# A table of 242 moves behind the planner's order of an attention and expert-layer kernel

## The chip, the cores and the metric

One core of one Trainium2 chip runs the whole program. The metric is the device time of one execution in microseconds (us), the median of several runs. TensorE (PE) does the matmuls, VectorE (DVE), ScalarE (ACT) and GpSimd (POOL) the rest of the arithmetic; SyncE (SP) issues every transfer of this kernel.

## The reference

Attention over 4 batches, 8 heads, 768 positions and 64 dimensions: each query sees its window of positions less than 16 away, and 24 blocks of 32 positions, by the largest key and the mean value of each. A gated layer over all 3072 tokens follows (512 to 1536 to 512).

```python
    k_sum = k.reshape(B, H, nb, block, D).max(axis=3)
    v_sum = v.reshape(B, H, nb, block, D).mean(axis=3)
    scale = 1.0 / np.sqrt(D)
    scores_l = scale * np.matmul(q, k.transpose(0, 1, 3, 2))
    mask_l = np.abs(pos[:, None] - pos[None, :]) < window
    scores_s = scale * np.einsum('bhsd,bhnd->bhsn', q, k_sum)
    scores_s = scores_s + np.log(block)
    scores_l_m = np.where(mask_l, scores_l, -1000000000.0)
    scores_all = np.concatenate([scores_l_m, scores_s], axis=-1)
    scores_all = scores_all - np.max(scores_all, axis=-1, keepdims=True)
    a = np.exp(scores_all)
    a = a / (np.sum(a, axis=-1, keepdims=True) + 1e-09)
    v_all = np.concatenate([v, v_sum], axis=2)
    return np.matmul(a, v_all).astype(np.float32)
...
    g = x @ w_gate
    silu = g * (1.0 / (1.0 + np.exp(-g)))
    val = x @ w_val
    return (silu * val @ w_out).astype(np.float32)
```

`block` is 32 and `window` 16; x is the output of the attention, one row for each token.

## The kernel before

Tokens are worked on in halves of a batch, 384 each: half k = 0 and 1 are batch 0, 2 and 3 are batch 1, and so on. A unit (k,u) is the attention of two heads (u = 0 to 3) in half k. Its steps carry names: SC(k,u) scores on TensorE; max, scl or ttr0 and ttr1 the row maxima with the mask on DVE; exp0 to exp5 on ScalarE; eps a tiny addition to the sums, rcp their reciprocal; nrm the product of probabilities and reciprocals (128x720, L708, on DVE or POOL); PP0 and PP1 the transposes on TensorE into PSUM, pt0 and pt1 their copies to SBUF; XO the product with the values (L762); xh and xl the split of x into a high and a low part, since every product of float32 is made of three matmuls of parts.

For half 0 the values come out of one tile vn of the values as they lie in memory. odd1(u) and odd2(u) copy shifted rows of it into the window tile vw, and val1(u) and val2(u) copy the block means (24 rows) into vw and vn; all four are copies of 384 columns (L465 on POOL or DVE, L463 on ACT) and XO(0,u) reads what they write. Later halves load windows of values, and values(k,u) copies the means into them (24x768); join does the same for keys, pool and vpool make the maxima and sums of blocks.

The weights of the expert layer arrive in 12 pieces each of gate and value together (w0 to w11) and of output (o0, o2, ...), as 64-bit floats that are decoded to float32: raw_w is the load (128x2048, 1024 KB), then abs (ACT, L941), clamp, shift, sign and low (DVE, L945 to L964, 128x1024), then hi (ACT, a cast, L463) and lo (DVE or POOL, the remainder, L468) for the matmuls. keep_w stores a decoded piece, wa, sf, la, ls and again_w are later transfers of weights and of sums. sumA22, sumA21, sumA12 and sumA11 are sums of 256-wide parts of a decoded piece (L468).

g(j,h) and v(j,h) are the gate and value matmuls of piece j for half h of batch 0 (L1105); silu, mul, hh and hl make the activation and its two parts, D0 and D1 multiply by the output weights, part adds up. Batches 1 to 3 use seven products of sums in place of eight plain ones (P1 to P7, L1147).

What sets the order: every operation is a Step of a Plan, with a cost on each engine that may do it. `order` (L273) works out when each step is wanted and lets `run` (L308) place the steps one by one; a table `NUDGES` shifts the wanted times by hand and names engines. In `run`, a step of POOL or DVE that doesn't read PSUM is held until 0.2 us before the end of such a step on the other of the two (`held`, L361 to L402). The steps come back sorted by their planned start, and the loop at L1469 issues them so; `after` chains each engine's instructions in this order. All transfers stand in one queue, that of SyncE. In the first 110 us of the plan, `warm_up` (L1257) puts up to 30 matmuls on a tile of zeros ahead of a TensorE step for which the plan shows idle time.

Of the kernel before, what the change touches and what calls it, by code (L numbers as in the profile page):

```python
# [80 lines left out]
PE, DVE, ACT, POOL, DMA = "PE", "d", "a", "p", "q"  # L81
# [174 lines left out]
def nudge(steps, late):  # L256

    by = {s.name.replace(" ", "_"): s for s in steps}
    for line in NUDGES.replace("\n", ";").split(";"):
        if not line.strip():  # L260
            continue
        name, *what = line.split()
        s = by[name]
        for x in what:
            if x[0] in "+-":
                late[s] += float(x)
            elif x[0] == "s":
                s.slack = float(x[1:])
            else:
                s.engines = {x: s.engines[x]}  # L270


def order(steps):  # L273

    for s in steps:
        s.next = []
    for s in steps:
        for o in s.after:
            o.next.append(s)
    pe = [s for s in steps if PE in s.engines]  # L280
    line = [[s for s in pe if s.side == x] for x in range(2)]
    wanted = {}
    t = 6.0
    for s in pe:
        wanted[s] = t
        t += s.engines[PE]
    for _ in range(3):
        late = {}
        for s in reversed(steps):
            x = wanted.get(s, 1e9)  # L290
            for o in s.next:
                x = min(x, late[o] - (LAG.get(o_engine(s), 0.07) if s.after is not None else 0))
            late[s] = x - min(s.engines.values(), default=0)
        run(steps, line, late)
        wanted = {s: s.start + s.engines[PE] for s in pe}
        for s in line[1]:
            if s.gate is not None:
                wanted[s] = min(wanted[s], s.gate.end + EARLY)
    nudge(steps, late)
    run(steps, line, late)  # L300
    return sorted(steps, key=lambda s: (s.start, s.n))


def o_engine(s):
    return next(iter(s.engines), None)
# [106 lines left out]
def body(ctx, tc, qP, kP, kW, vT, vW, vN, vR, wgv, wo, bias, out):  # L412
    nc = tc.nc

    def after(x, y):

        tc.add_manual_dep(
            x, y.name, mybir.DependencyInfo(mybir.DependencyClass.NoSync, mybir.DependencyReason.DATA), reason="order"
        )
# [10 lines left out]
    def make(buf):  # L430
        if buf.tile is None:
            buf.tile = pools[buf.ring.pool][1].tile(
                buf.shape, buf.dtype, tag=buf.ring.tag, bufs=buf.ring.bufs, name=buf.name
            )
        return buf.tile
# [9 lines left out]
    plan = Plan()  # L445
# [27 lines left out]
    spare = [0]  # L473
# [66 lines left out]
    KT, KS, VT, VR, Q, KWD, VW, PR, PT, ST, XO, VN = ({} for _ in range(12))  # L540
# [538 lines left out]
    def silu(name, a, src, reads):  # L1079
        plan.add(  # L1080
            name, {ACT: 0.49}, lambda e: nc.scalar.activation(out=make(a), in_=src(), func=AF.Silu), reads, (a,), table="silu"  # L1081
        )
# [383 lines left out]

    traced = nc.cur_bb.bb.instructions
    last = {}
    for s in order(plan.steps):  # L1469
        if s.engine == PE and s.start < 110.0:  # L1470
            spare[0] = min(30, max(0, int((s.idle - 0.5) / 0.25)))
        n = len(traced)
        if s.engine is None:
            s.do()
        else:
            s.do(s.engine)
        spare[0] = 0
        for x in traced[n:]:
            if x.engine in last:
                after(x, last[x.engine])  # L1480
            last[x.engine] = x
# [45 lines left out]
```

## Time and profile before

| what | us |
|---|---|
| median of 3 runs | 677.97 |
| lowest and highest | 676.67, 678.21 |
| the profiled execution | 678.46 |
| its span | 676.8 |
| TensorE busy in it | 662.9 |
| DVE busy in it | 498.9 |

The profiled execution is one run like the others, taken with the hardware profiler. Its span goes from the first to the last instruction; 1.66 us of its time lie around it. An engine's busy time counts its instructions, so idle time of TensorE is what the order around it can change.

### The profile page before, as it was taken

The page shows a single profiled execution, that of the slowest core. Times are in us where ns is not written, and L with a number is a line of the kernel's source. Part 1 is how long each engine was busy: PE and PEld are TensorE (multiplying, and loading weights), DVE is VectorE, ACT ScalarE, POOL GpSimd, SP SyncE. Part 2 cuts the span into 40 slices and gives each one's busy share as a digit, 9 for nine tenths or more (in the row PEclk, how much of TensorE's full clock was granted, in tenths as well). Part 3 has the DMA queues.
Part 4 walks back from the last instruction along what each step waited for, and adds up shares of the span by engine and source line. Part 5 has one row for each costly group of instructions (what it writes and reads, how often), then busy time and mean ns, then how long its engine had stood idle before and what let it go on. Part 6 is the DMA issues. An engine that isn't in the chain of part 4 may idle for free.

```text
span 676.8 us, 13318 instructions
## 1 busy us (share of the span) xinstructions
PE 662.9 (98%) x5077; PEld 611.0 (90%) x5077; DVE 498.9 (74%) x1073; ACT 373.5 (55%) x901; POOL 130.7 (19%) x141
## 2 busy tenths in 40 slices
PE   8799999999999999999999999999999999999997
PEld 8699899899898899989898998989999898989896
DVE  5899998999979685967689674766658761646464
ACT  4877758868654576545645386754635243413130
POOL 4303113235225020145413100201003000000000
PEclk9999999999999999999999999999999999999999
DMA  9997668869964686886657484663726362626232
GB/s 345 365 383 283 221 242 284 289 234 354 324 227 167 254 305 222 315 284 219 241 205 253 155 303 150 222 214 112 249 72 211 144 251 73 239 88 222 106 110 93
DMA packets 39681, 152.71 MB, mean 226 GB/s; under 512 B 4352, under 2 KB 8896, under 8 KB 32704
## 3 DMA queue, kind: packets, MB, share of 16 engines
q1 hardware_dynamic: 39616, 151.85, 63.3%
q8 instruction: 40, 0.66, 0.4%
q14 instruction: 25, 0.20, 0.1%
HBM read 116.18 MB, written 35.65 MB: 224 GB/s over the span
## 4 chain that ended last, share of the span: by engine, by line
PE 84%; DMA 8%; DVE 5%; SPq 1%; ACT 1%; issue 1%; POOL 0%; DVEq 0%; POOLq 0%
PE p L1147 35%; PE acc L1219 28%; PE g L1105 6%; PE v L1105 6%; DMA s<-ss 3%; PE xo L762 3%; DMA raw_o<-in_wo 3%; PE pp L729 2%; PE sc L610 2%; DMA s<-sf 1%; DMA vn<-in_vN 1%; SPq L482 1%; DVE p L708 0%; DVE nm L663 0%; DVE o L468 0%
## 5 line engine op out<-in xcount | busy, mean ns | idle before, releaser
L1219 PE MATMUL acc<-o,hh 128*128 128x512 f32 x570 | 178.0, 393 | 0.0
L1219 PEld LDWEIGHTS acc<-o,hh 128*128 128x128 f32 x570 | 105.4, 188 | 22.1 <-issue 1.3
L1147 PE MATMUL p<-xh_T,s 128*128 128x384 f32 x432 | 122.5, 338 | 0.9 <-DMA s<-ss 0.8
L1219 PE MATMUL acc<-o,hl 128*128 128x512 f32 x285 | 111.5, 391 | 0.0
L1147 PE MATMUL p<-xh_B,wa 128*128 128x384 f32 x288 | 84.9, 335 | 0.0
L1147 PEld LDWEIGHTS p<-xh_T,s 128*128 128x128 f32 x432 | 79.0, 188 | 3.2 <-DMA s<-ss 2.0
L463 ACT CAST hh<-a 128x384 fp32r<-128x384 f32 x73 | 37.5, 514 | 70.1 <-DVE a L468 67.3
L463 ACT COPY s<-p 128x384 f32<-128x384 f32 x64 | 30.7, 479 | 75.5 <-PE p L1147 75.1
L1147 PE MATMUL p<-xl_T,s 128*128 128x384 f32 x216 | 72.3, 335 | 0.0
L468 DVE TENSOR_TENSOR part<-acc,part 128x512 f32<-128x512 f32 x71 | 47.2, 684 | 27.0 <-PE acc L1219 27.0
L1219 PEld LDWEIGHTS acc<-o,hl 128*128 128x128 f32 x285 | 53.5, 188 | 11.8 <-DVE hl L468 0.3
L468 DVE TENSOR_TENSOR hl<-a,hh 128x384 fp32r<-128x384 f32 x84 | 49.3, 586 | 14.0 <-ACT hh L463 11.2
L653 ACT ACTIVATE p<-p,nm 128x120 f32<-128x120 f32 x144 | 55.1, 384 | 2.5 <-DVE nm L641 2.2
L468 DVE TENSOR_TENSOR c<-p,u 128x384 f32<-128x384 f32 x72 | 39.7, 552 | 22.7 <-PE p L1147 22.6
L1105 PE MATMUL g<-xh_B,w 128*128 128x384 f32 x192 | 53.7, 338 | 0.0
L1105 PE MATMUL v<-xh_B,w 128*128 128x384 f32 x192 | 53.4, 337 | 0.0
L1147 PEld LDWEIGHTS p<-xh_B,wa 128*128 128x128 f32 x288 | 53.0, 188 | 0.1
L1147 PE MATMUL p<-xl_B,wa 128*128 128x384 f32 x144 | 48.1, 334 | 0.0
L1147 PE MATMUL p<-xh_B,s 128*128 128x384 f32 x144 | 42.6, 336 | 1.0 <-DVE v L468 1.0
L1147 PE MATMUL p<-xh_T,wa 128*128 128x384 f32 x144 | 42.3, 334 | 0.0
L468 DVE TENSOR_TENSOR a<-c,a 128x384 f32<-128x384 f32 x65 | 36.2, 557 | 7.1 <-ACT a L1081 4.1
L1147 PEld LDWEIGHTS p<-xl_T,s 128*128 128x128 f32 x216 | 40.6, 188 | 0.3
(161 smaller groups left out, 1353.3 us busy)
## 6 DMA issues: line engine op xcount, KB each, us to landing
wa<-wa SPq DMA_DIRECT2D x36, 768.0 KB, 4.3
s<-ss SPq DMA_DIRECT2D x24, 1024.0 KB, 7.3
raw_w<-in_wgv SPq DMA_DIRECT2D x12, 1024.0 KB, 7.4
ss<-s SPq DMA_DIRECT2D x12, 1024.0 KB, 7.2
wa<-w SPq DMA_DIRECT2D x12, 768.0 KB, 6.0
kw<-in_kW SPq DMA_DIRECT2D x24, 360.0 KB, 5.6
vw<-in_vW SPq DMA_DIRECT2D x28, 288.0 KB, 4.6
kt<-in_kP SPq DMA_DIRECT2D x16, 400.0 KB, 5.4
```

Of the source, the lines that this page charges most:

```text
L463: nc.scalar.copy(out, in_)
L468: vector[e].tensor_tensor(out=out, in0=a, in1=b, op=op)
L482: plan.add(name, {DMA: moved(name, nbytes)}, lambda e: nc.sync.dma_start(out(), in_()), reads, writes)
L610: nc.tensor.matmul(make(sc[h])[s * QT : (s + 1) * QT, c * KC + at : c * KC + at + x.shape[-1]], make(q)[hs, qs], x, start=not biased or c ...
L653: nc.scalar.activation(out=make(p)[:, i, :], in_=make(p)[:, i, :], func=AF.Exp, scale=-1.0, bias=make(nm)[:, i : i + 1], accum_out=make(sm ...
L729: nc.tensor.transpose(make(pp)[:KC, c * P : (c + 1) * P], make(p)[:, g * NT // 2 + c, :], make(id_sb))
L762: nc.tensor.matmul(ps[hs, qs], v, make(pt)[:, h, qs], start=True, stop=True)
L1105: nc.tensor.matmul(t[:, :TOK], a, x, start=u == order_of[0] and i == 0, stop=u == order_of[-1] and i == 2,)
L1147: nc.tensor.matmul(t[:, :TOK], a, x, start=first and kk == 0 and n == 0, stop=kk == 1 and n == 2, skip_group_check=not first,)
L1219: nc.tensor.matmul(ps[:, :wide], a, w, start=j == js[0] and m == 0, stop=j == js[-1] and m == 2)
```

## The change

After the planner has its order, `moved_behind` takes each engine's list of steps out of it and goes through a table of 242 pairs: of a pair `x y`, step x is taken out of its engine's list and put directly behind y. 102 pairs are on DVE, 54 on ScalarE, 44 in the transfer queue, 21 on TensorE and 21 on POOL; no step changes its engine, and nearly all belong to the first third of the run. Then one common order is made of the lists again, by rank and by what each step needs. The rule for warm-up matmuls is replaced by a table: 14 of them instead of 21, at SC(0,1), PP0(0,2) and PP1(0,2). No step is added, removed or computed in another way. ScalarE's order has 44 table loads in place of 46, because steps that use the same table stand together more often. The lines of the functions below the table are 75 higher in the changed kernel.

```diff
+WARM = {"SC(0,1)": 5, "PP0(0,2)": 8, "PP1(0,2)": 1}
+
+MOVES = (
...
+    "vpool(1,3) part(0,1,5); mul(6,0) sign_w8; vpool(2,0) mul(6,0); hh(0,6,0) vpool(2,0); low_w8 low_w9; "
...
+    "odd2(2) val2(0); val2(2) odd2(2); val1(2) val2(2); values(1,1) eps(1,1); sumA22_w3 eps(1,3); sumA11_w2 sumA22_w3; "
...
+)
+
+def moved_behind(out):
+
+    lists = {}
+    for i, s in enumerate(out):
+        s.rank = i
+        lists.setdefault(s.engine, []).append(s)
+    named = {s.name.replace(" ", "_"): s for s in out}
+    for pair in MOVES.split("; "):
+        x, y = (named[n] for n in pair.split())
+        line = lists[x.engine]
+        line.remove(x)
+        line.insert(line.index(y) + 1, x)
+    marks = set(lists.pop(None, []))
+    done, again = set(), []
+    while marks or any(lists.values()):
+        heads = [l[0] for l in lists.values() if l] + list(marks)
+        s = min((h for h in heads if all(o in done for o in h.after)), key=lambda h: h.rank)
+        if s.engine is None:
+            marks.remove(s)
+        else:
+            lists[s.engine].pop(0)
+        done.add(s)
+        again.append(s)
+    return again
...
-    for s in order(plan.steps):
-        if s.engine == PE and s.start < 110.0:
-            spare[0] = min(30, max(0, int((s.idle - 0.5) / 0.25)))
+    for s in moved_behind(order(plan.steps)):
+        if s.engine == PE:
+            spare[0] = WARM.get(s.name, 0)
```

The first place is the transfer queue at the start. In a row, `kt`, `q` and `vn` are keys, queries and values of half 0, `raw_w0` to `raw_w3` weight pieces, `vw_1_0` window values of half 1. Before:

```order
L482 DMA kt_0_2_229<-in_kP 128x800
L482 DMA raw_w0_234<-in_wgv 128x2048
L482 DMA raw_w3_299<-in_wgv 128x2048
L482 DMA q_0_2_320<-in_qP 128x384
L482 DMA raw_w1_333<-in_wgv 128x2048
L482 DMA vw_1_0_371<-in_vW 96x768
L482 DMA vw_1_1_376<-in_vW 96x768
L482 DMA raw_w2_416<-in_wgv 128x2048
```

Changed:

```order
L557 DMA kt_0_2_223<-in_kP 128x800
L557 DMA raw_w0_228<-in_wgv 128x2048
L557 DMA vn0_230<-in_vN 128x1536
L557 DMA vn0_230<-in_vR 32x256
L557 DMA q_0_2_310<-in_qP 128x384
L557 DMA raw_w1_316<-in_wgv 128x2048
L557 DMA vw_1_0_351<-in_vW 96x768
L557 DMA raw_w2_356<-in_wgv 128x2048
```

The load of piece w3 has left this place: it stands behind raw_w2, the load raw_o0 and the store keep_w1, seven rows below the end of this list. The values vn0 now come behind piece w0.

The second place is POOL from about 15 to 31 us. `vw_0_u` and `vn` are the value tiles of unit (0,u) and `vs_0` the block means, so `vw_0_2<-vn1` is odd2(2), `vw_0_2<-vs_0` val1(2), `vn1<-vs_0` val2(2), `vw_0_0<-vs_0` val1(0) and `vn0<-vs_0` val2(0); the row of L708 is nrm(0,2). Before:

```order
L465 COPY vw_0_2_323<-vn1_119 32x384
L465 COPY vw_0_2_323<-vs_0_296 24x384
L465 COPY vn1_119<-vs_0_296 24x3x128
L465 COPY vw_0_1_255<-vs_0_296 24x384
L465 COPY vw_1_1_376<-vs_0_296 24x768
L465 COPY vw_0_0_464<-vn0_184 64x384
L465 COPY vw_0_0_464<-vn0_184 32x384
L465 COPY vw_0_0_464<-vs_0_296 24x384
L465 COPY vn0_184<-vs_0_296 24x3x128
L708 TENSOR_TENSOR p_0_2_468<-p_0_2_468,ri_0_2_518 128x720
```

Changed:

```order
L540 COPY vw_0_3_321<-vn1_116 32x384
L540 COPY vw_0_0_442<-vn0_230 32x384
L540 COPY vw_0_3_321<-vs_0_293 24x384
L540 COPY vn1_116<-vs_0_293 24x3x128
L783 TENSOR_TENSOR p_0_2_449<-p_0_2_449,ri_0_2_503 128x720
L540 COPY vw_0_0_442<-vs_0_293 24x384
L540 COPY vn0_230<-vs_0_293 24x3x128
L540 COPY vw_0_2_490<-vn1_116 32x384
L540 COPY vn1_116<-vs_0_293 24x3x128
L540 COPY vw_0_2_490<-vs_0_293 24x384
```

val1(0), val2(0) and the three copies of unit (0,2) stood ahead of nrm(0,2) and now stand behind it; those of unit (0,3) follow odd2(0) at the top of the second list.

The third place is DVE at about 146 to 153 us, around the decoding of pieces w8 and w9. `m_w9<-raw_w9` of the last two decode lines are sign and low, `w8<-m_w8` is lo w8, `vw_3_0<-vs_1` values(3,0), and the ISA rows are ttr0(3,0). Before:

```order
L964 SCALAR_TENSOR_TENSOR m_w8_1847<-raw_w8_1553,m_w8_1847 128x1024
...
L468 TENSOR_TENSOR w8_1990<-m_w8_1847,w8_1990 128x1024
L468 TENSOR_TENSOR hl_0_6_1_2015<-a_0_6_1_1926,hh_0_6_1_2008 128x384
L468 TENSOR_TENSOR a_0_7_0_2013<-v_7_0_1993,a_0_7_0_2013 128x384
L951 TENSOR_SCALAR m_w9_1970<-m_w9_1970 128x1024
L465 CAST hh_0_7_0_2034<-a_0_7_0_2013 128x384
L958 SCALAR_TENSOR_TENSOR m_w9_1970<-raw_w9_1633,m_w9_1970 128x1024
L832 TENSOR_REDUCE vr_2_0_2054<-vt_2_0_1853 128x24
L964 SCALAR_TENSOR_TENSOR m_w9_1970<-raw_w9_1633,m_w9_1970 128x1024
L465 COPY vw_3_0_2071<-vs_1_1646 24x768
L641 ISA p_3_0_2124,nm_3_0_2125<-sc0_3_0_2074,bias_sb_825 128x120
```

Changed:

```order
L1033 SCALAR_TENSOR_TENSOR m_w9_1955<-raw_w9_1657,m_w9_1955 128x1024
L1039 SCALAR_TENSOR_TENSOR m_w9_1955<-raw_w9_1657,m_w9_1955 128x1024
L1039 SCALAR_TENSOR_TENSOR m_w8_1819<-raw_w8_1505,m_w8_1819 128x1024
L543 TENSOR_TENSOR a_0_7_0_2013<-v_7_0_1972,a_0_7_0_2013 128x384
L540 COPY vw_3_0_2106<-vs_1_1636 24x768
L716 ISA p_3_0_2109,nm_3_0_2110<-sc0_3_0_2052,bias_sb_807 128x120
...
L543 TENSOR_TENSOR w8_2085<-m_w8_1819,w8_2085 128x1024
```

low w8 has gone from eleven rows ahead of low w9 to the row behind it, and lo w8 from ahead of the steps of w9 to behind values(3,0) and ttr0(3,0). On POOL, hl(0,7,0) stood ahead of lo w9 and is now behind it.

## Rows read from the trace of the kernel before

**Rows 1.** The page: the span, TensorE's busy time, the clock granted to TensorE in 40 equal slices (tenths of full speed), and the chain of work that ended last, by engine.

```profile
span 676.8 us, 13318 instructions
...
PE 662.9 (98%) x5077; PEld 611.0 (90%) x5077; DVE 498.9 (74%) x1073; ACT 373.5 (55%) x901; POOL 130.7 (19%) x141
...
PEclk9999999999999999999999999999999999999999
...
PE 84%; DMA 8%; DVE 5%; SPq 1%; ACT 1%; issue 1%; POOL 0%; DVEq 0%; POOLq 0%
```

**Rows 2.** Busy time by stretch: the stretch, its length, busy time and instructions of TensorE, its weight loads, DVE, ACT and POOL, TensorE's granted clock, the share of the transfer engines, GB/s.

```profile
0.00:36.50 36.50, 29.87 (x471) 26.79 (x472) 27.67 (x50) 24.68 (x78) 13.65 (x28) 1.00 0.97 359
36.50:75.00 38.50, 37.38 (x446) 33.95 (x445) 37.83 (x60) 31.29 (x82) 10.90 (x10) 1.00 0.82 303
...
151.00:162.00 11.00, 11.00 (x115) 10.77 (x110) 10.87 (x35) 10.69 (x27) 5.50 (x6) 1.00 0.96 320
...
220.40:245.00 24.60, 23.60 (x174) 22.73 (x173) 18.20 (x56) 16.46 (x41) 4.50 (x6) 1.00 0.75 266
```

**Rows 3.** TensorE's waits from 0 to 245 us: the waiting line, what it waited for, us in total, how often, the longest.

```profile
PE pp L1260 <- ACT pt L463: 1.9, 1, 1.9
PE sc L610 <- DMA q<-in_qP: 1.4, 2, 0.9
...
PE p L1147 <- DVE v L468: 1.0, 1, 1.0
...
PE pp L729 <- DVE p L708: 0.7, 1, 0.7
```

**Rows 4.** The timeline around lo w9 and values(3,0) and (3,1): start and length in us, engine, line, operation, shape. The first POOL row is another step of the same shape (lo w6).

```profile
152.43 0.56 DVE L465 COPY vw<-vs 24x768 f32<-24x768 f32 x1
154.96 2.05 DVE L465 COPY vw<-vs 24x768 f32<-24x768 f32 x1
...
126.55 2.41 POOL L468 TENSOR_TENSOR w<-m_w,w 128x1024 fp32r<-128x1024 f32 x1 [7.25 <-ACT w L463]
153.99 2.59 POOL L468 TENSOR_TENSOR w<-m_w,w 128x1024 fp32r<-128x1024 f32 x1 [2.73 <-ACT w L463]
```

**Rows 5.** The timeline of POOL's copies of values and of nrm(0,2), and DVE's low w0, from 20 to 31 us.

```profile
20.52 0.69 POOL L465 COPY vw<-vs 24x384 f32<-24x384 f32 x1 [3.32 <-ACT vs L463]
22.05 1.06 POOL L465 COPY vw<-vn 64x384 f32<-64x384 f32 x1
23.16 1.39 POOL L465 COPY vw<-vn 32x384 f32<-32x384 f32 x1
25.06 0.51 POOL L465 COPY vn<-vs 24x384 f32<-24x384 f32 x1
29.47 1.39 POOL L708 TENSOR_TENSOR p<-p,ri 128x720 f32<-128x720 f32 x1 [3.90 <-DVE ri L705]
...
22.66 1.52 DVE L964 SCALAR_TENSOR_TENSOR m_w<-raw_w,m_w 128x1024 int32<-128x1024 int32 x1
```

**Rows 6.** The page's row of the loads of gate and value pieces (KB each, us from issue to landing), and the timeline of rcp(0,2), of the decoding after it (clamp w2), of XO(0,2)'s second part and of the first matmul of g(0,0).

```profile
raw_w<-in_wgv SPq DMA_DIRECT2D x12, 1024.0 KB, 7.4
...
29.13 0.19 DVE L705 RECIPROCAL ri<-sm 128x6 f32<-128x6 f32 x1
33.68 0.69 DVE L945 TENSOR_SCALAR m_w<-m_w 128x1024 f32<-128x1024 f32 x1 [1.41 <-ACT m_w L941]
...
34.45 0.27 PE L762 MATMUL xo<-pt,vw 120*64 120x64 f32 x1
35.28 0.44 PE L1105 MATMUL g<-xh_B,w 128*128 128x384 f32 x1
```

**Rows 7.** The view of the decoded pieces' tile on POOL (the 256-wide sums: shortest, median and longest in ns), and the timeline of rcp(1,3) and of POOL's hl for another step.

```profile
L468 POOL TENSOR_TENSOR m_w<-m_w x9: 729/1250/1713, 55.3 to 105.0; 128x256 f32<-128x256 f32 x9
...
71.78 0.19 DVE L705 RECIPROCAL ri<-sm 128x6 f32<-128x6 f32 x1
...
67.84 1.01 POOL L468 TENSOR_TENSOR hl<-a,hh 128x384 fp32r<-128x384 f32 x1 [2.50 <-ACT hh L463]
```

**Rows 8.** The timeline of ScalarE's abs w1, hi w5, a table load and an exponential, of DVE's lo w5, and of the first matmul of g(5,0).

```profile
23.94 1.15 ACT L941 ACTIVATE m_w<-raw_w 128x1024 f32<-128x1024 f32 x1 [1.10 <-DMA raw_w<-in_wgv]
...
99.47 1.06 ACT L463 CAST w<-m_w 128x1024 fp32r<-128x1024 f32 x1 [2.89 <-DVE m_w L964]
103.47 1.28 ACT L653 ACT_TABLE_LOAD   x1
104.76 0.40 ACT L653 ACTIVATE p<-p,nm 128x120 f32<-128x120 f32 x1
...
101.08 1.21 DVE L468 TENSOR_TENSOR w<-m_w,w 128x1024 fp32r<-128x1024 f32 x1
...
107.84 0.33 PE L1105 MATMUL g<-xh_B,w 128*128 128x384 f32 x1
```

**Rows 9.** The timeline of DVE's lo w8, low w9 and the first of three parts of ttr0(3,0), and of the first matmul of g(8,0).

```profile
146.13 1.21 DVE L468 TENSOR_TENSOR w<-m_w,w 128x1024 fp32r<-128x1024 f32 x1
151.18 1.21 DVE L964 SCALAR_TENSOR_TENSOR m_w<-raw_w,m_w 128x1024 int32<-128x1024 int32 x1
153.02 0.28 DVE L641 CUSTOM_DVE_ANT_0 p<-sc,bias_sb 128x120 f32<-128x120 f32 x1
...
154.91 0.33 PE L1105 MATMUL g<-xh_B,w 128*128 128x384 f32 x1
```

41 rows, old and new, of the table MOVES are left out of this document.

## The prediction

> **What bounds the kernel now.** I read the page first: TensorE is busy for 662.9 of 676.8 us, at a granted clock of 9 tenths or more in every slice (the higher of its two levels, 2.4 GHz), and the chain that ended last is 84% TensorE, with transfers second at 8% and VectorE (DVE) third at 5% [rows 1]. So the time can only change where TensorE waits. The busy times by stretch show where that is. From 0 to 36.5 us TensorE is busy 29.87 us; part of the rest is the start, before the first data. From 36.5 to 75 it lacks 1.12 us, from 75 to 220.4 nothing (the stretch 151 to 162 stands for it), and from 220.4 to 245 just 1.00 [rows 2]. TensorE's waits name what was late: 1.9 us before the transposes of unit (0,2), 0.7 for the probabilities of (1,3), 1.0 for one value product at 236 us, 1.4 in all for queries q [rows 3]. The moves lie in the first third, so they can win at most the waits in this list that they touch, and they can lose wherever a step that had time to spare now has none. DVE is the engine to watch: busy 37.83 of 38.50 us in the second stretch and 10.87 of 11.00 in 151 to 162, almost as full as TensorE [rows 2].
>
> **A price that the sum needs.** GpSimd (POOL) and DVE hold each other up in this kernel. A copy 24x768 on DVE took 0.56 us at 152.43 and 2.05 at 154.96, while POOL's lo w9 ran from 153.99 to 156.58 [rows 4]. On POOL a copy of values took 0.51 us alone, but 1.06 (64x384) and 1.39 (32x384) beside DVE's low w0 of 22.66, which itself took 1.52 [rows 5] where the same step on w9 took 1.21 [rows 9]. I read this as one waiting until about 0.13 us before the other ends (154.96+2.05 = 157.01 is POOL's end 156.58 plus 0.56 less 0.13). So a POOL copy that meets a 1.21-us decode step costs up to 1.39 - 0.51 = 0.88 us. The planner's run keeps such steps apart when it places them (the `held` times); the moves are made after it and ask no such thing.
>
> The Trainium skill ("SBUF — State Buffer", section "Who interferes with whom") calls the port pair that DVE and GpSimd share an exclusive lock, held for the whole instruction. The rows above agree (2.05 against 0.56 us); by that rule an order chosen with step times that stay as profiled misjudges every new meeting, and by its opposite the terms 2 and 4 below would be near 0.
>
> **The change part by part**, all against the profiled run (678.46 us; span 676.8).
>
> Term 1, up to the first gate matmul g(0,0) at 35.28 us. The load raw_w3 leaves the queue ahead of q(0,2) and raw_w1. It is 1024 KB, 1.05 MB, at the 359 GB/s of this stretch 2.9 us [rows 2, 6]. Scores, exponentials and rcp(0,2) (29.13) can be that much earlier; xh(1,0) and xl(1,0), some 0.5 each, are now ahead of them on DVE and take one such slot back: 2.4 earlier. So nrm(0,2) on POOL begins at 29.47 - 2.4 = 27.1 and ends 1.39 later, at 28.5 [rows 5, 6]. But behind it POOL now has five copies, val1(0), val2(0), odd2(2), val2(2), val1(2), which stood before it and were done by 25.6 [rows 5]. Alone they take 5 x 0.5 = 2.5. DVE has decode steps there (lo w0, sign w1, low w1, clamp w2, clamp o0), so I let three meet steps of 1.21 at 0.88 each, and two meet shorter steps at 0.4 each, between 0.69 - 0.51 = 0.2 (20.52) and 1.06 - 0.51 = 0.55 [rows 5]: 3.4. The last ends at 28.5 + 2.5 + 3.4 = 34.4, and a handover later, at 34.5, XO(0,2) has what it needs; from 34.45, where its second part begins, to 35.28 it took 0.83 [rows 6]; 34.5 + 0.83 = 35.3. **+0.1**: the whole gain of the queue is spent on the copies. Bounds: -2.9 if no copy meets DVE; +1.1 if all five cost 0.88. val1(3), val2(3) are also behind six other POOL copies now, ahead of XO(0,3); TensorE waits there instead, up to 2.3 us by the same prices, but upstream of the same point.
>
> Term 2, 36 to 75 us. POOL now does sumA22 w3 between eps(1,3) and what follows, 0.729 us at its shortest, while DVE does rcp(1,3) (0.19) and wants nrm(1,3): it waits 0.73 - 0.19 - 0.13 = 0.4, and PP0(1,3) already waits 0.7 for it, so all of it is on the path [rows 3, 7]. nrm(1,1) is moved behind lo w3 and rcp(1,1), beside POOL's hl(0,1,0); the like hl at 67.84 took 1.01: 0 to 0.9, I take 0.6, since DVE has 0.67 us idle in 38.5 and can't make it up [rows 2, 7]. **+1.0** [0 to 1.7, to allow for a longer sum].
>
> Term 3, g(5,0) at 107.84. It needs lo w5, which ended at 102.29, a reserve of 5.5 us. hi w5 (99.47, after 2.89 of idle) is now behind seven exponentials (0.4 each), two table loads (1.28 each), abs o8 (1.15, as abs w1 took) and silu(4,0), which came right after it (about 0.5): 2.8 + 2.6 + 1.15 + 0.5 = 7.0 of ScalarE work less 0 to 2.9 of idle, so 103.6 to 106.5; with hi 1.06, a handover of 0.1 and lo 1.21, 106.0 to 108.9 against 107.84 [rows 8]. **+0.6** [0 to 1.1], nearer the late end because abs o8 now also waits for raw_o8, moved back on the queue.
>
> Term 4, g(8,0) at 154.91. It needs lo w8, which ended at 147.34 and had 7.6 us to spare; now low w8 stands behind low w9, and lo w8 behind values(3,0) and ttr0(3,0). POOL's lo w9 began 1.6 us after low w9's end (152.39 to 153.99), behind hi w9. Call that end X. DVE then does low w8 (1.21) and mul(7,0) (0.56), and wants values(3,0) at X + 1.77, when lo w9 has run 0.17: held until X + 1.6 + 2.41 - 0.13 = X + 3.88. Then values 0.56, ttr0 0.6 (three of 0.28, overlapping), lo w8 1.21: X + 6.25 [rows 4, 9]. Counted from where low w9 ended, X is 150.0 if both steps that left from ahead of it (2 x 1.21) are won, 151.2 if one, because the other's place goes to waiting for TensorE's v(7,0): 156.2 to 157.4. **+1.8** [0 to 2.5], the middle of +1.3 to +2.5. If lo w9 comes just after values, it meets lo w8 instead and costs 0.5 less. Without a meeting it is X + 4.14, at most 155.3: +0.4 or nothing.
>
> Term 5, 236 us: the 1.00 us wait for a value product sits behind DVE work that is moved: **-1.0** [-1.0 to 0] [rows 3].
>
> At nothing: the 21 TensorE moves (same matmuls, other order); the other transfers, whose cover is a transfer share of 0.75 to 0.97 [rows 2] (a late one would show as a new wait on a DMA); seven fewer warm-up matmuls, which run only inside waits; two fewer table loads, on an engine half idle. Beyond some 250 us the order stays as it was.
>
> Sum: 0.1 + 1.0 + 0.6 + 1.8 - 1.0 = +2.5, so 680.96 beside the profiled 678.46. That run is 0.49 above the median of 677.97: **680.5 us**.
>
> **The rivals.** (A) Faster: POOL and DVE miss each other. It is decided by lo w9 starting late enough for values(3,0) and lo w8 to be past, and by the copies behind nrm(0,2) falling into DVE's gaps. Terms: -2.9, 0, 0, 0, -1.0 = -3.9, 674.1; half of term 1 kept gives 676. For it: DVE waited 1.41 us for data before 33.68, so there are gaps [rows 6]; against: a share of 37.83 in 38.50 leaves few [rows 2]. (B) No change: the copies cost what they won, but lo w9 misses values(3,0), and terms 2 and 3 are halved: 0.1 + 0.5 + 0.3 + 0 - 1.0 = -0.1, 677.9. (C) Slower still: the longer wait before XO(0,3), 2.3 us against 1.9 as the longest so far, lets the clock fall. In the trace it stayed at 1.00 after 1.9 us [rows 2, 3], which speaks against it. Some 5 us of matmuls at half rate add 3 to 5: 684 to 686. The Trainium skill ("TensorE: Matmul & The Clock Gate", part 1) says that an idle array is throttled to half its clock; no run here shows it in this kernel.
>
> **How the numbers follow.** My forecast has 0.59, A 0.27, B 0.10, C 0.04. A has that much because all terms but the fifth hang on when POOL and DVE meet, and half a microsecond decides each meeting. The upper bounds of the terms with term 5 lost give 1.1 + 1.7 + 1.1 + 2.5 = +6.4, 684.4; they won't all come together, and the range ends at 684.0. Below, it takes in B and the half-way form of A, to 675.0, and leaves out the rest of A (about 0.13) and C. A measurement here can tell about 0.2% (1.36 us) from no change: 676.6 to 679.3 is the same. Faster 0.27 (A), same 0.10 (B), slower 0.63.
>
> **What would show it.** Term 1: in the trace of the changed kernel nrm(0,2) on POOL about 2.4 us earlier, the five copies behind it at 0.9 to 1.5 us each, g(0,0) within 0.5 of 35.3; if the copies take 0.5, A is right. Term 2: nrm(1,3), of 128x720 elements, some 0.4 longer than nrm(1,1) alone. Term 3: a TensorE wait on lo w5 before g(5,0). Term 4: values(3,0) or lo w8 over 2 us long beside lo w9, and a TensorE wait for w8 before g(8,0), the largest new one after 40 us. Term 5: no wait of 1.0 at 236. I am wrong if POOL's and DVE's steps keep their lengths, or if a wait on a transfer stands in the list of TensorE's waits after 40 us.

## The result and the profile after

The changed kernel takes 683.11 us (681.53 to 684.11, 4 runs) where the kernel before takes 677.51 (4 runs): a ratio of 1.0080, with a 95% interval of 1.0062 to 1.0099. In a second group of runs it was 1.0081 (1.0063 to 1.0099). It is slower, by 5.6 us; the forecast was 680.5, or 2.5 us slower, less than half of the measured change.

The profiled execution took 684.11 us, its span is 682.4. The page shows, as in [rows 1], the span, TensorE's busy time, its granted clock by slice, and the chain that ended last, by engine:

```profile
span 682.4 us, 13274 instructions
...
PE 665.3 (97%) x5063; PEld 612.6 (90%) x5063; DVE 507.3 (74%) x1073; ACT 370.2 (54%) x899; POOL 135.5 (20%) x141
...
PEclk9979999999999999999999999999999999999999
...
PE 85%; DVE 8%; ACT 3%; DMA 1%; POOL 1%; issue 1%; DVEq 0%; ACTq 0%; POOLq 0%
```

TensorE is busy 2.4 us longer with fewer matmuls (5063 against 5077), which already says that some of them ran slower: the third slice has a clock of 7 tenths. In the chain, VectorE has gone from 5% to 8% and transfers from 8% to 1%.

TensorE's waits from 0 to 250 us, the counterpart of [rows 3], in us in total, times, longest:

```profile
PE xo L837 <- POOL vn L540: 5.8, 3, 2.8
PE g L1180 <- DVE w L543: 2.1, 2, 1.4
PE pp L804 <- DVE p L783: 1.7, 1, 1.7
...
PE sc L685 <- DMA q<-in_qP: 0.7, 1, 0.7
...
PE xo L837 <- POOL vw L540: 0.4, 1, 0.4
```

The wait of 1.9 before PP0(0,2), the 1.0 at 236 us and both waits for q are gone. New are waits for POOL's copies (6.2 us), for decoded weights (2.1) and for another q (0.7, at 92 us), and the wait for the probabilities of (1,3) has grown from 0.7 to 1.7. Where they lie, POOL first: nrm(0,2) and the five copies behind it (start, length), against [rows 5]:

```profile
27.57 1.39 POOL L783 TENSOR_TENSOR p<-p,ri 128x720 f32<-128x720 f32 x1 [1.85 <-DVE ri L780]
29.02 1.38 POOL L540 COPY vw<-vs 24x384 f32<-24x384 f32 x1
30.35 1.50 POOL L540 COPY vn<-vs 24x384 f32<-24x384 f32 x1
31.91 1.38 POOL L540 COPY vw<-vn 32x384 f32<-32x384 f32 x1
33.35 0.85 POOL L540 COPY vn<-vs 24x384 f32<-24x384 f32 x1
34.15 0.96 POOL L540 COPY vw<-vs 24x384 f32<-24x384 f32 x1
```

nrm(0,2) starts 1.9 us earlier than in [rows 5], and the copies take 6.07 us together, where alone they would take 2.5.

The second place, rcp(1,3) and nrm(1,3) on DVE beside POOL's sums, then nrm(1,3) of the kernel before (L708); after that, in the changed kernel, lo w9 on POOL with values(3,0) and lo w8 on DVE, and the first matmul of g(8,0), against [rows 4, 9]:

```profile
75.35 0.19 DVE L780 RECIPROCAL ri<-sm 128x6 f32<-128x6 f32 x1 [1.62 <-POOL sm L777]
75.58 1.32 DVE L783 TENSOR_TENSOR p<-p,ri 128x720 f32<-128x720 f32 x1
...
75.40 2.09 POOL L543 TENSOR_TENSOR m_w<-m_w 128x256 f32<-128x256 f32 x2
...
72.00 0.91 DVE L708 TENSOR_TENSOR p<-p,ri 128x720 f32<-128x720 f32 x1
...
157.78 2.41 POOL L543 TENSOR_TENSOR w<-m_w,w 128x1024 fp32r<-128x1024 f32 x1 [9.48 <-ACT w L538]
...
158.20 2.40 DVE L540 COPY vw<-vs 24x768 f32<-24x768 f32 x1
161.25 1.22 DVE L543 TENSOR_TENSOR w<-m_w,w 128x1024 fp32r<-128x1024 f32 x1
...
162.52 0.44 PE L1180 MATMUL g<-xh_B,w 128*128 128x384 f32 x1 [1.44 <-DVE w L543]
```

values(3,0) takes 2.40 us where it took 0.56, lo w8 ends at 162.47, and TensorE, which waited 1.44 for it, starts g(8,0). nrm(1,3) takes 0.4 us longer than before, but it also starts late: DVE had waited 1.62 us for POOL's eps, the sums that rcp(1,3) reads.

The clock by short stretches (columns as in [rows 2]):

```profile
32.00:34.00 2.00, 0.83 (x24) 0.69 (x24) 2.00 (x3) 1.04 (x2) 1.94 (x2) 1.00 0.12 49
34.00:36.00 2.00, 1.31 (x20) 1.12 (x22) 2.00 (x3) 0.38 (x2) 1.12 (x2) 0.55 1.01 315
38.00:39.00 1.00, 1.00 (x5) 1.00 (x4) 1.00 (x2) 0.00 (x0) 0.00 (x0) 0.50 0.96 321
41.00:42.00 1.00, 1.00 (x49) 0.97 (x42) 0.62 (x1) 0.86 (x2) 0.00 (x0) 0.99 0.95 393
```

After the waits for the copies TensorE runs at its lower level of 1.2 GHz from 34 to 41 us, with work all the time from 36 on. The kernel before has 1.00 there in its profiled run [rows 2].

The last two columns, the transfers, change too. The load raw_w3 now stands behind the store keep_w1, which waits for DVE's low w1 (its end is at 32.93). Between 24.4 and 32.95 us the one queue issues nothing. Below are two stretches of the changed kernel, one of the kernel before, then keep_w1 and raw_w3 in the changed kernel's queue, and ScalarE's wait for raw_w3:

```profile
28.00:30.00 2.00, 2.00 (x21) 2.00 (x20) 2.00 (x3) 1.98 (x4) 1.94 (x2) 1.00 0.06 23
30.00:32.00 2.00, 0.46 (x6) 0.22 (x6) 1.97 (x3) 1.90 (x4) 1.94 (x3) 1.00 0.00 0
...
28.00:30.00 2.00, 0.48 (x4) 0.48 (x5) 2.00 (x5) 1.43 (x8) 0.53 (x1) 1.00 0.98 395
...
32.95 0.33 SPq L557 DMA_DIRECT2D whole<-m_w  x1
33.33 0.42 SPq L557 DMA_DIRECT2D raw_w<-in_wgv  x1
...
ACT m_w L1016 <- DMA raw_w<-in_wgv: 3.3, 1, 3.3
```

ScalarE's abs w3 waits 3.3 us for the load. No wait of TensorE comes from it in this trace, but one can be followed to it in e8_repair (below).

By stage, the starts of single steps in the changed kernel and in the one before: g(0,0) 36.44 and 35.28 (+1.15), g(1,0) 46.99 and 43.71 (+3.28), g(0,1) 77.64 and 73.66 (+3.98), v(5,0) 115.73 and 109.92 (+5.81), v(8,0) 164.71 and 156.99 (+7.73), and at 252 us +7.4. Later 1.8 of that comes back, in a part whose order is the same, where the profiled run of before waited 0.8 us for loads of sums and that of after did not.

### The profile page after: what moved, and what is told of

Read it like the earlier page. It is cut to its first block, busy times and chain, and to the rows that moved or that the text cites. A ratio compares the mean times of both kernels' runs of the same rounds, so it can differ in the third digit from the quotient of the medians.

```text
span 682.4 us, 13274 instructions
## 1 busy us (share of the span) xinstructions
PE 665.3 (97%) x5063; PEld 612.6 (90%) x5063; DVE 507.3 (74%) x1073; ACT 370.2 (54%) x899; POOL 135.5 (20%) x141
## 4 chain that ended last, share of the span: by engine, by line
PE 85%; DVE 8%; ACT 3%; DMA 1%; POOL 1%; issue 1%; DVEq 0%; ACTq 0%; POOLq 0%
PE p L1222 37%; PE acc L1294 27%; PE g L1180 5%; PE v L1180 4%; PE xo L837 3%; PE sc L685 3%; PE pp L804 2%; DMA vt<-in_vT 1%; DVE p L783 1%; DVE w L543 1%; DVE m_w L1039 1%; PE dummy L1342 1%; DVE o L543 1%; ACT p L752 1%; POOL vw L540 1%
```

## The experiments

The ratios stand against runs of the kernel before in the same group; its median was 677.51 beside the changed kernel, 676.64 beside e1 to e4, 676.41 beside e5 to e8 and 677.46 beside e9 to e11, so medians of different groups are not to be compared. An interval is 1 to 3 us wide, so a difference of 1 us between two rows is not resolved.

| kernel | median us | ratio | interval |
|---|---|---|---|
| changed | 683.11 | 1.0080 | 1.0062 to 1.0099 |
| e9_again (the same again) | 682.43 | 1.0081 | 1.0063 to 1.0099 |
| e1_warm | 681.21 | 1.0065 | 1.0051 to 1.0079 |
| e3_lo9 | 681.63 | 1.0074 | 1.0059 to 1.0089 |
| e5_copies | 681.35 | 1.0084 | 1.0065 to 1.0103 |
| e8_repair | 680.16 | 1.0059 | 1.0044 to 1.0074 |
| e11_repair2 | 680.80 | 1.0052 | 1.0033 to 1.0071 |
| e4_raw3 | 677.28 | 1.0009 | 0.9998 to 1.0021 |
| e6_bwarm | 675.91 | 0.9996 | 0.9988 to 1.0005 |
| e7_raw3warm | 677.48 | 1.0015 | 1.0003 to 1.0027 |
| e10_raw3b | 677.11 | 1.0001 | 0.9979 to 1.0022 |

e2_short has one run (680.75) and leaves work out; only its trace counts.

**Does the clock cost anything?** e1_warm:

```diff
-WARM = {"SC(0,1)": 5, "PP0(0,2)": 8, "PP1(0,2)": 1}
+WARM = {"SC(0,1)": 5, "XO(0,3)": 9, "PP0(0,2)": 8, "PP1(0,2)": 1, "XO(0,0)": 4, "XO(0,2)": 4}
```

> The changed kernel with 17 more warm-up matmuls: 9 ahead of XO(0,3), 4 ahead of XO(0,0), 4 ahead of XO(0,2), where TensorE waits for POOL's copies. Theory: the waits of 2.8, 1.5 and 1.4 us brought the granted clock down to its lower level (0.50 from 35 to 41 us), and what that costs comes on top of the late copies. Then the clock stays at 1.00 in 34 to 41 us, the copies on POOL stay as long as they are (0.85 to 1.5 us each), and g(1,0) starts 1.8 to 2.6 us earlier than the 46.99 of the changed kernel; in all 680.5 to 681.5 instead of 683.1. Rival: the slow stretch was hidden behind weights that were late anyway; then the clock stays up and g(1,0) is within 0.5 us of 46.99, in all 683.

The clock in its trace, same columns:

```profile
34.00:36.00 2.00, 1.42 (x27) 1.22 (x26) 1.70 (x3) 0.40 (x1) 0.69 (x1) 1.00 1.06 317
36.00:38.00 2.00, 2.00 (x20) 1.75 (x21) 1.89 (x3) 0.08 (x1) 0.00 (x0) 1.00 0.94 351
38.00:41.00 3.00, 3.00 (x66) 2.71 (x60) 3.00 (x4) 1.47 (x2) 0.00 (x0) 1.00 1.05 337
```

The clock stays up, POOL's five copies last as long as before (1.38, 1.50, 1.38, 0.85, 0.96), and g(1,0) starts at 43.99, 3.0 us earlier. Of this 2.4 are left at 252 us. With the clock kept, g(0,0) starts at 35.48, 0.20 later than in the kernel before: that is what the moves themselves cost in the first stage, as far as one profile tells. In the timed runs the gain looks smaller, 1.0080 to 1.0065 (1.0 us), but the intervals overlap. The profiled run of the changed kernel is the longest of its four, and its mean clock (0.995) is below that of two of them (0.997).

**Are the copies long because they meet DVE?** e2_short leaves five decode steps on 64 of 1024 columns:

```diff
+SHORT = {"sign w1": 64, "low w1": 64, "clamp w2": 64, "clamp o0": 64, "shift w2": 64}
...
+        c = {x: SHORT.get(f"{x} {name}", n) for x in ("clamp", "shift", "sign", "low")}
+        low = lambda: make(raw).rearrange("p (n t) -> p n t", t=2)[:, : c["low"], 0]
```

> The changed kernel in which five decode steps of DVE (sign w1, low w1, clamp w2, clamp o0, shift w2) work on 64 columns of 1024, so these parts of the weights stay undecoded; the order, the transfers and ScalarE's steps are the same. Theory: the copies on POOL behind nrm(0,2) are long because they meet these steps. Then val1(0) still takes 1.4 us beside lo w0, the other four 0.50 to 0.55 each instead of 1.50, 1.38, 0.85 and 0.96, XO(0,2) starts about 2 to 2.7 us earlier than 34.26 and g(0,0) 2.5 to 3.5 earlier than 36.44. Rival: transfers or ScalarE's copies make POOL slow; then the four copies stay at 0.85 to 1.5 us and g(0,0) within 0.5 us of 36.4.

POOL behind nrm(0,2), and DVE's lo w0 and the first of the short steps:

```profile
28.88 1.38 POOL L542 COPY vw<-vs 24x384 f32<-24x384 f32 x1
30.21 0.51 POOL L542 COPY vn<-vs 24x384 f32<-24x384 f32 x1
30.77 0.50 POOL L542 COPY vw<-vn 32x384 f32<-32x384 f32 x1
31.34 0.51 POOL L542 COPY vn<-vs 24x384 f32<-24x384 f32 x1
31.79 0.51 POOL L542 COPY vw<-vs 24x384 f32<-24x384 f32 x1
...
28.29 1.60 DVE L545 TENSOR_TENSOR w<-m_w,w 128x1024 fp32r<-128x1024 f32 x1
29.82 0.52 DVE L1037 SCALAR_TENSOR_TENSOR m_w<-raw_w,m_w 128x64 int32<-128x64 int32 x1
```

This settles it for the four: the one copy beside a full step (lo w0) takes 1.38, the four others 0.50 to 0.51. The last ends at 32.3 in place of 35.1. XO(0,2) starts only 0.7 us earlier, though, not the 2 to 2.7 expected, and g(0,0) 2.1 earlier: here the clock fell sooner, after the wait of 2.6 us ahead of XO(0,3) (0.50 from 26 to 30 us), and the eight warm-up matmuls and transposes of (0,2) took 3.7 us (PP0(0,2) at 28.44, PP1(0,2) at 32.15) where the changed kernel took 2.2 (27.46, 29.65).

**lo w9 off POOL.** e3_lo9 lets a move change the engine, and adds one:

```diff
+        lists[x.engine].remove(x)
+        x.engine = y.engine
         line = lists[x.engine]
-        line.remove(x)
...
+    "lo_w9 lo_w8"
```

> The changed kernel with one more move: lo w9 is taken from POOL and put behind lo w8 on DVE, so POOL has nothing beside values(3,0). Theory (POOL and DVE hold each other up): values(3,0) takes 0.56 us instead of 2.40, lo w8 ends 1.8 us earlier, the wait of 1.4 us before g(8,0) goes, g(8,0) comes 1.4 to 1.8 us earlier against the stage before it (XO(2,3) to v(8,0): 6.5 to 6.9 us instead of 8.35); lo w9 adds 1.2 us to DVE, which is before g(9,0) wanted, and up to 0.8 us of the gain is lost there: in all 0.7 to 1.6 below the changed kernel. Rival: values(3,0) was long because its source or its tile was late or because of ScalarE; then it stays at 2.4 us and nothing is won.

```profile
157.78 0.56 DVE L543 COPY vw<-vs 24x768 f32<-24x768 f32 x1
```

That is values(3,0) on DVE: 0.56 again. From XO(2,3) to v(8,0) it is 6.87 us in place of 8.35 (1.5 won), then from v(8,0) to g(9,0) 23.80 in place of 23.07, 0.7 lost; a wait of 0.28 for hl, a step of DVE, which now does lo w9 too, is in it, and the rest was not followed. Term 4's meeting stands. The kernel before takes 6.49 from XO(2,3) to v(8,0), though, so 0.38 is left that has nothing to do with it. In the timed runs the difference (1.0074 to 1.0081) is below what they can tell.

**Copies on ScalarE.** e5_copies adds to the changed kernel (with the engine rule of e3_lo9):

```diff
+    "val2(0) pt1(0,0); val2(2) abs_w2; val2(3) abs_w1"
```

> The changed kernel with three of POOL's copies put on ScalarE, where it is idle: val2(3) behind abs w1, val2(0) behind pt1(0,0), val2(2) behind abs w2. Theory (the copies on POOL are what spent the gain of the queue): XO(0,3) starts 1 to 1.5 us earlier than 25.77, XO(0,2) 1.8 to 2.5 us earlier than 34.26, g(0,0) 1.8 to 3 us earlier than 36.44; if the shorter waits keep the clock up, g(1,0) comes 4 us earlier than 46.99, otherwise 2. In all 679.5 to 681.5. Rival: another step is as late (xl(0,0), lo w0 or nrm(0,2)); then g(0,0) moves by less than 0.7 us and the total stays at 682 to 683.

XO(0,3) starts at 24.48 (1.3 earlier, as expected), XO(0,2) at 33.47 (0.8 earlier, short of the 1.8), g(0,0) at 34.69 (1.75 earlier), g(1,0) at 43.21 (3.8 earlier). TensorE's waits for POOL's copies have gone, but ScalarE's copies of transposes are next:

```profile
PE xo L840 <- ACT pt L541: 3.5, 3, 1.8
...
26.00:28.00 2.00, 2.00 (x14) 1.88 (x12) 1.64 (x5) 1.97 (x8) 0.39 (x1) 0.50 0.93 361
```

and the clock again falls, from 25 to 28 us. The timed runs show no gain (1.0084, interval as wide as that of the changed kernel), though the profiled execution is 2.4 us shorter than that of the changed kernel. So the copies were late, and moving them handed a part of the wait on.

**The first stage's gain alone.** e4_raw3 is the kernel before with one move:

```diff
-MOVES = (
...
+MOVES = (
+    "raw_w3 keep_w0"
 )
```

> The kernel before with a single move: the load raw_w3 behind the store keep_w0, and the warm-up matmuls as they were (21). Theory: the loads q(0,2), raw_w1, raw_o0 and raw_w2 come 2.9 us earlier; POOL's copies stay where they were, ahead of nrm(0,2); nrm(0,2) itself gains only some 0.3 us, since DVE has its old order, but abs o0 on ScalarE, which waited 1.6 us for raw_o0 ahead of pt1(0,0), no longer does, and g(0,0) comes 1.3 to 2.0 us earlier than 35.28; 0.5 of that is lost again by 75 us. In all 0.8 to 1.8 us below the kernel before, 675.7 to 676.7. Rival: w3 is then late itself, or the gain at g(0,0) is used up before 75 us; then no change (677.5).

No change (1.0009). Its clock also fell, to 0.60 and 0.54 of full speed in 30 to 34 us, behind a wait of 2.0 us. So two more kernels fill that wait with warm-up matmuls, without the move and with it:

```diff
-WARM = {"SC(0,1)": 5, "PP0(0,1)": 3, "XO(0,1)": 2, "XO(0,3)": 3, "PP0(0,2)": 8}
+WARM = {"SC(0,1)": 5, "PP0(0,1)": 3, "XO(0,1)": 2, "XO(0,3)": 3, "PP1(0,0)": 7, "PP0(0,2)": 8}
```

The first line is what the rule of the kernel before gives.

> The kernel before, its order untouched, with 7 more warm-up matmuls, ahead of PP1(0,0), so that TensorE works through the wait of 1.9 us ahead of PP0(0,2). Theory: most runs of the kernel before also lose a little to the clock in the first 45 us (mean granted clock 0.996 to 0.999 of the 12 latest runs, 1.00 in the one profiled first), so the clock now reads 1.000 in all runs and the time is 0.5 to 1.2 us below the kernel before: 675.4 to 676.1. Rival: the loss lies elsewhere in the run, or PP1(0,0) behind the warm-up matmuls delays ScalarE; then no change or up to 0.5 us slower.

> The single move of raw_w3 behind keep_w0, with the same 7 more warm-up matmuls ahead of PP1(0,0). Theory: the single move gained 1.1 to 1.7 us at g(0,0) but lost it to the clock (0.54 to 0.60 of full speed from 30 to 34 us in its trace), so with the warm-up matmuls g(0,0) comes at 33.5 to 34.2 instead of 35.14 and the total is 1.0 to 2.2 us below the kernel before: 674.5 to 675.6. Rival: the wait of TensorE only moves elsewhere (nrm(0,2) still starts at 29.5); then g(0,0) stays at 35 and the total is that of the kernel before less what its clock lost.

e4_raw3's g(0,0) came at 35.14, not 1.3 to 2.0 earlier. e6_bwarm keeps a mean clock of 0.999 to 1.000 in 10 of 11 runs; of the 22 runs of the kernel before beside it, 11 are at 0.996 or 0.997. The time is 0.9996 of before (0.9988 to 1.0005): 0.5 us less in the medians, within the interval of no change. e7_raw3warm has the expected gain at g(0,0), 33.22 against 34.79 in e6_bwarm, and then loses all of it and 0.8 more before PP0(1,0), at 50.28 against 49.52. The reason stands on DVE at 42 us and on TensorE at 50:

```profile
42.39 0.70 DVE L978 TENSOR_SCALAR m_w<-m_w 128x1024 f32<-128x1024 f32 x1 [2.67 <-ACT m_w L974]
...
50.28 0.44 PE L762 MATMUL pp<-id_sb,p 128*120 128x128 f32 x1 [2.15 <-DVE p L741]
```

clamp w3 waits 2.67 us, as abs w3 waited for a raw_w3 that was put behind a store, and everything behind it on DVE, nrm(1,0) among it, is late. Behind TensorE's wait of 2.15 the clock falls too, to 0.55 from 50 to 52 us and 0.60 from 52 to 54. Six of its twelve runs have a mean clock of 0.996 or 0.997 and take 678.2 to 679.5 us, the other six have 0.998 to 1.000 and take 675.9 to 676.8. So the rival of e4_raw3's expectation holds, and the clock adds to it. Would it help if w3 were in time?

```diff
-    "raw_w3 keep_w0"
+    "raw_w3 raw_o0"
```

> The order of the kernel before with the 7 more warm-up matmuls ahead of PP1(0,0), and raw_w3 put only behind raw_o0 (still ahead of keep_w0, so that it isn't held up by that store). Theory: what made the single move useless was that raw_w3 landed so late that DVE waited 2.7 us for w3 at 42 us, ahead of nrm(1,0); here w3 is in time, no such wait stands, and what q(0,2) and raw_w1 win remains: 0 to 1.0 us below the same kernel without the move, 674.9 to 675.9, if the kernel before is at 676.4. Rival: nothing on the way to g(0,0) waits for q(0,2) or raw_w1 alone (nrm(0,2) stands behind DVE's own steps); then it is the same as with the warm-up matmuls alone.

There is no such wait on DVE, and no gain either: g(0,0) at 34.90, nrm(0,2) at 29.98 (30.09 in e6_bwarm), ratio 1.0001. That nothing on the way waits for these loads, as the rival says, is not shown: in e7_raw3warm, with DVE's order as untouched as here, nrm(0,2) came at 29.29 (its last keys for half 0 also landed earlier, at 13.20 against 14.43). What the trace of e10_raw3b shows is that the store keep_w0, here still behind raw_w3, lands at 31.96, in e7_raw3warm at 29.88, and that abs w2 on ScalarE, which writes the tile that is stored, waits for it:

```profile
32.06 1.21 ACT L974 ACTIVATE m_w<-raw_w 128x1024 f32<-128x1024 f32 x1 [0.95 <-DMA whole<-m_w]
```

So raw_w3 is itself late behind keep_w0, and ahead of it keeps that store late.

**All repairs.** e8_repair, and e11_repair2 with one move more:

```diff
+    "val2(0) pt1(0,0); val2(2) abs_w2; val2(3) abs_w1; lo_w9 lo_w8; sumA22_w3 join(2,0); "
+    "sumA11_w2 sumA22_w3; sumA12_w3 sumA11_w2"
...
+    "hi_w5 silu(4,0)"
```

> The changed kernel with all repairs together: the three copies on ScalarE, lo w9 on DVE behind lo w8, the sums A22 w3, A11 w2 and A12 w3 on POOL behind the copy join(2,0) instead of ahead of nrm(1,3), and 13 more warm-up matmuls ahead of XO(0,3), XO(0,0) and XO(0,2). Theory: the terms add up (clock 2.4, copies 1.9, w9 1.2, nrm(1,3) 0.4: 5.9, less some 0.7 that comes back at later waits), so the kernel returns to the time of the kernel before or close to it: 676.5 to 678.5. Rival: the terms overlap, because behind each wait another one stands, and it stays above 679.5.

> The kernel with all repairs, and hi w5 taken from behind exp5(2,0) to directly behind silu(4,0), ahead of the table load. Theory of term 3 (g(5,0) waits for hi w5 and lo w5 behind the table load and exp5): the wait of 0.68 us before g(5,0) is gone, v(5,0) comes 0.5 to 0.8 us earlier against v(4,1) (4.4 us behind it instead of 5.1), and the total is 0.2 to 0.7 below the kernel with the other repairs: 0.45 to 0.6% above the kernel before. Rival: lo w5 is late because of DVE's own queue; then the wait stays.

> The changed kernel once more, as it is, beside the kernels of this group, so that their ratios stand against the same runs of the kernel before. Expected: 0.6 to 1.0% above the kernel before, with a mean granted clock of 0.995 to 0.997 in every run. If the slow stretch of the clock were chance, some of its runs would show 1.000 and be 2 us shorter.

e8_repair reaches 1.0059 (680.16), not the kernel before: the rival holds, the terms overlap. g(0,0) comes at 34.22, 2.2 earlier than in the changed kernel, but PP0(1,0) at 50.32, no earlier than in e1_warm (50.23): nrm(1,0) on DVE stands there, and TensorE waits 1.16 for it. Before that DVE waited 1.05 for abs w3 ahead of clamp w3 (first row), because raw_w3 still stands behind keep_w1, and it has no idle time from there to nrm(1,0). nrm(1,3) takes 0.91 again, and PP0(1,3) waits 1.30 where e1_warm has 1.67; the view puts this down to a copy of partial sums on ScalarE, which ends at 73.92, but nrm(1,3) ends at 73.91:

```profile
41.97 0.69 DVE L1024 TENSOR_SCALAR m_w<-m_w 128x1024 f32<-128x1024 f32 x1 [1.05 <-ACT m_w L1020]
...
50.32 0.84 PE L808 MATMUL pp<-id_sb,p 128*120 128x128 f32 x6 [1.16 <-DVE p L787]
...
74.06 0.84 PE L808 MATMUL pp<-id_sb,p 128*120 128x128 f32 x6 [1.30 <-ACT part L542]
```

e11_repair2 confirms term 3: v(5,0) comes 4.34 us behind v(4,1), against 5.11, and the wait of 0.68 before g(5,0) is gone. Its ratio of 1.0052 is not distinguishable from that of e8_repair. e9_again repeats the changed kernel: mean clock 0.995 to 0.997 in all six runs, none at 1.000, so the fall is no chance of one profile.

## Why the prediction was right, and where it was short

The sign and the mechanism held: POOL and DVE meet where they did not before, and the steps that were taken at their profiled times are longer in the new order. The size was less than half of what was measured, and some terms came out at their forecast by luck. By its terms:

- **Term 1**, +0.1 at g(0,0): measured with the clock kept, +0.20 (e1_warm). The five copies were put at 5.9 us, and took 6.07; nrm(0,2) came 1.9 earlier, not 2.4. e2_short shows the cause, not only the time. That the sum fits to 0.1 us is luck: in e9_again, the same kernel, g(0,0) comes 1.0 us later than in the first profile, behind a wait of 1.45 for its first queries. The Trainium skill ("SBUF — State Buffer", section "Who interferes with whom") says that the port pair of the two engines is an exclusive lock and, of a VectorE instruction in its two-port modes, that whoever issues first has it for the whole instruction while the other is fully blocked; of one with two inputs in SBUF, as lo, sign and low are, it says only that it contends with a GpSimd instruction that reads SBUF. The copies of 1.38 to 1.50 beside lo w0, sign w1 and low w1, and of 0.51 beside no full step, agree.
- **Term 2**, +1.0: from g(1,0) to g(0,1) the kernel before takes 29.95 us, e1_warm 30.99: +1.04, and the changed kernel 30.65: +0.70. Of the two parts that were named, nrm(1,3) is 1.32 for 0.91 as forecast, and e8_repair, where it is 0.91 again, gets 0.37 of the wait before PP0(1,3) back. nrm(1,1) is 1.50 for 0.89 as forecast, and two waits of TensorE of 0.3 behind it in e1_warm can be its. But the wait before PP0(1,3) grew by 0.94, and the half of it that isn't nrm(1,3)'s has another cause: DVE, which the term had without idle time, waited 1.62 us just before rcp(1,3), for sums that ScalarE's exponentials give. Those start 5.4 us after the scores of (1,3) are done, 4.4 in the kernel before, and no term has that; on the other side a wait of 0.39 that the kernel before has in this stretch is gone. So that the sum agrees to 0.04 is in part luck.
- **Term 3**, +0.6: the wait before g(5,0) is 0.65 in the changed kernel and goes with hi w5's place (e11_repair2).
- **Term 4**, +1.8: XO(2,3) to v(8,0) takes 8.35 us for 6.49, +1.86. values(3,0) was held as computed, and e3_lo9 takes it away. But the wait was 1.44, and e3_lo9 wins 1.48; the other 0.38 stays without it. It lies in TensorE's own time, so part of this agreement is luck too.
- **Term 5**, -1.0: in the two profiled runs it came true (P6(1,1) to P3(1,1) 6.38 for 7.53). But the order of before has 6.37 there in e6_bwarm, and 6.56 in e4_raw3 with one load moved, with no such wait. The 1.0 us belonged to one execution, not to the order, so this step failed: a wait in one profile was booked as a gain of the moves.
- **The clock**, rival C, was wrongly taken as something in place of the forecast and given 0.04. It came on top: 2.4 us between the traces of the changed kernel and e1_warm. What failed is the sentence that the clock stayed up after a wait of 1.9 us, which was read as evidence against a fall after 2.3. That wait became 2.84, and the clock was still at 1.00 until 34 us; it fell after two more waits for copies, of 1.54 and 1.43.
- **"At nothing"** failed in three places. q(2,0), moved back behind raw_w4, made SC(2,0) wait 0.71 us in the changed kernel's profile and 0.90 in e1_warm's, but not in e9_again's: it is part of the time in some executions. The 21 TensorE moves are not free: from g(0,1) to v(5,0) the changed kernel takes 38.08 us with waits of 1.36, the kernel before 36.27 with none, for the same 255 matmuls, so 0.45 is added in TensorE's own time (0.43 in e9_again); from v(5,0) to v(8,0) it is 0.47 (48.98 with a wait of 1.44, against 47.07). And the cover of the other transfers, a share of 0.75 to 0.97, became 0.06 and 0.00 from 28 to 32 us.

At v(8,0) the changed kernel is 7.73 us behind. By these rows terms 1 to 4 are 3.3 of it (0.2, 1.0, 0.65 and 1.44; forecast 3.5), the clock 2.4, q(2,0) 0.7 and TensorE's own time 0.9, 7.3 in all. What the forecast lacked is thus the last three, and term 5 counted a gain that was none. This sum was made afterwards, from single profiles.

What stays open: why e8_repair, with the clock up and three of the terms repaired, is still 4 us above the kernel before. Part of it can be placed. TensorE is busy 2.1 us longer in it than in e6_bwarm, with two matmuls less and with the clock at 1.00 in both up to their last matmuls (the page of e8_repair, then of e6_bwarm):

```profile
PE 666.1 (98%) x5089; PEld 612.6 (90%) x5089; DVE 503.2 (74%) x1074; ACT 372.0 (55%) x902; POOL 130.5 (19%) x137
...
PE 664.0 (99%) x5091; PEld 613.0 (91%) x5091; DVE 498.0 (74%) x1073; ACT 373.1 (55%) x901; POOL 130.4 (19%) x141
```

The rest is waits (1.16 for nrm(1,0) behind the late raw_w3, 1.30 before PP0(1,3), 0.68 for w5). Only the last was taken away by itself (e11_repair2). Neither TensorE's old order nor raw_w3 ahead of keep_w1 was run with the repairs, so what they are worth is not shown. No kernel here beats the one before beyond the interval: the best, e6_bwarm, is at 0.9996.

## What to carry to other kernels

An order chosen by replaying step times holds only as long as the steps keep their times: where two engines hold each other up, as POOL and DVE do here, move a step only with a look at what runs beside it on the other, and price each new meeting with the rest of the other's instruction. A wait found in one profiled run is a gain to be had only if other executions show it. In a single transfer queue a load that is put behind a store waits for what the store waits for: raw_w3 was late behind keep_w0 and behind keep_w1, and ahead of keep_w0 it kept that store late. And a term that agrees in size is not yet shown: look at whether the wait named by it is the one that stood there.

## What the runs showed of the hardware that was not expected

The granted clock halved in this kernel after TensorE had waited 2.84, 1.54 and 1.43 us (0.50 from 36 to 41 us, although TensorE was busy all of that time), after 2.6 us in e2_short, and behind waits of 2.0 in e4_raw3, 2.15 in e7_raw3warm and 1.8 in e5_copies; behind 1.9 in the profiled run of before it stayed at 1.00, and yet 11 of 22 later runs of that kernel have a mean of 0.996 or 0.997, as the profiled runs of e4_raw3, e5_copies and e7_raw3warm have with such a fall. So it seems to fall in some executions of the kernel before too; no trace of one was kept. Warm-up matmuls in the wait kept it up (e1_warm, and 10 of 11 runs of e6_bwarm). After a fall, eight warm-up matmuls and the first transposes of (0,2) took 3.7 us in place of 2.2 (e2_short).
